# Lightning attention into a gated feed-forward: the state update of block 1 moved behind the second attention output group, its decayed k made in two pieces

## The chip, the cores and the metric

The kernel runs on one core of a Trainium2 chip. The metric is the device time of one execution in microseconds (us). A core has five engines that run their own instruction streams in order and wait for one another by semaphores: TensorE (PE in the profile, its weight loads PEld), VectorE (DVE), ScalarE (ACT), GpSimd (POOL) and SyncE (SP). Here POOL also issues all loads from memory, and SP the output stores and the transposing transfers.

## The reference

Causal linear attention with a decay per head, then a feed-forward layer with a sigmoid gate. There are 4 batches, 8 heads, 768 positions, head width 64. The reference walks over the positions in blocks of 64 and carries a state of 64 x 64 per batch and head:

```
intra    = (qb kb^T * Dmask) vb          # Dmask[i,j] = lam^(i-j), j <= i
inter    = (qb * lam^(i+1)) kv_state
out      = intra + inter
kb_dec   = kb * lam^(block-1-pos)
kv_state = lam^block * kv_state + kb_dec^T vb
```

The attention output, laid out as 3072 tokens x 512, goes through `(sigmoid(x Wg) * (x Wv)) Wo` with 1536 hidden columns. The output is 3072 x 512 in float32.

## The kernel before, in words

The kernel takes blocks of 128 positions (C = 128), so there are six steps n = 0 to 5, and each handles all four batches: 512 tokens. All matrix work is in bf16, accumulated in float32. Work is written by hand as a list of pieces; on every engine the instructions run in exactly the order in which the pieces are written (`manual_schedule`), so the order of the calls is the schedule.

For one step the pieces are these. `load` brings q, k, v into the tiles Q, K, V (POOL issues; L84 in blocks 0 and 1, where k and q arrive per pair of batches, L78 for q and k of later blocks). `t` transposes q and k: for block 1 on PE (L159), then q is scaled by the decay into QS on DVE (L185) and k copied into KS by ACT (L223); from block 2 on, the transposes are transfers that SP issues (L176) into QR and KR. `sc` makes the scores q kT for two batches (L235), and `m` multiplies them by the decay mask on DVE (L252). `a` makes the attention output for one pair of batches: the part from the state `Sb` (L268), the part inside the block (L256), and two copies by ACT into XT, the feed-forward's input (L282). `make_kd` multiplies k by its decay on POOL (L300 for blocks 0 and 1, L306 later). `fade` makes the decayed old state `SD` on POOL (L315). `c` updates the state of one pair of batches: 16 small matmuls (L330) of the decayed k with v into a PSUM tile `cp`, then DVE adds `SD` and writes `Sb` (L337; a plain copy, L335, in block 0). `gv` is one of the twelve 128-column slices of the feed-forward's first layer: four matmuls for the gate (L346), a sigmoid on ACT (L349), four matmuls for the value (L352), and their product on DVE (L355). `gvh` is the same for half of the tokens, that is for one pair of batches (L363, L366, L369, L373). `piece_po` is the second layer for one batch (L391), copied by ACT and stored by SP.

PSUM has two rotating sets of banks: five (`ps_at`, tag "ps") for attention pieces, three (`ps_ff`, tag "ff") for the feed-forward. The update of batches 0 and 1 takes its `cp` from the first set, that of batches 2 and 3 from the second, where it stands in line with the gate and value tiles of `gvh`: a new tile of that set waits for the reader of the tile three places before it.

Feed-forward pieces of step n are interleaved with attention pieces of step n+1, to keep PE busy while other engines finish. Around the change (L462 to L490) that is: five `gv` of block 0; state update of block 0; `fade` and `make_kd(1)`; more `gv` of block 0 with the attention of block 1's first pair; the state update of that pair, `c(1, 0)`; the last `gv` of block 0; then the attention of the second pair, between `gvh` pieces of the first. POOL's own order there is: loads of block 1, the output weights, `fade`, `make_kd(1)`, loads of block 2, `fade`, `make_kd(2)`, loads of block 3. So whatever `make_kd(1)` waits for holds up the loads of block 2 behind it. Block 1's k of batches 2 and 3 is loaded by a transfer of its own (`load(1, "qk", 2, 4)`).

Of the kernel before, what the change touches and what calls it, by code (L numbers as in the profile page):

```python
# [11 lines left out]
ALU = mybir.AluOpType  # L12
# [4 lines left out]
def kernel(  # L17
# [11 lines left out]
    nc = tc.nc  # L29

    B, H, S, D = q.shape
# [8 lines left out]
    NB2 = B // 2  # L40
# [28 lines left out]
    Q, K, V = {}, {}, {}  # L69
# [68 lines left out]
    kds = const.tile([128, H], FP32, tag="kds")  # L138
# [5 lines left out]
    for u in range(2):  # L144
        nc.vector.tensor_tensor(
            out=mask[:, u].rearrange("p (e x) c -> p e x c", e=2),
            in0=tri.unsqueeze(1).unsqueeze(1).to_broadcast([128, 2, 2, C]),
            in1=pk.rearrange("p (x u e) -> p u e x", u=2, e=2)[:, u].unsqueeze(3).to_broadcast([128, 2, 2, C]),
            op=ALU.mult)

    def half(e):
        return slice(e * 64, (e + 1) * 64)

    def head(g, u):
        return 4 * (g % 2) + 2 * u + g // 2
# [12 lines left out]
    QS, KS, MT, XT, KD = {}, {}, {}, {}, {}  # L168
# [128 lines left out]
    def make_kd(n):  # L297
        if n < 2:
            KD[n] = kdp.tile([128, B, H, D], BF16, tag="kd", name="kd")
            nc.gpsimd.tensor_tensor(  # L300
                out=KD[n], in0=K[n],
                in1=kds.unsqueeze(1).unsqueeze(3).to_broadcast([128, B, H, D]), op=ALU.mult)
            return
        KD[n] = kdp.tile([128, 2, B, HP, D], BF16, tag="kd", name="kd")
        for e in range(2):
            nc.gpsimd.tensor_tensor(  # L306
                out=KD[n][:, e], in0=K[n][:, e],
                in1=kds[:, e::2].unsqueeze(1).unsqueeze(3).to_broadcast([128, B, HP, D]), op=ALU.mult)
# [10 lines left out]
    def kdh(n, b, h):  # L319
        return KD[n][:, b, h, :] if n < 2 else KD[n][:, h % 2, b, h // 2, :]  # L320

    def c(n, *pairs):
        for bp in pairs:
            pool, tag = (ps_at, "ps") if bp == 0 else (ps_ff, "ff")
            cp = pool.tile([128, 2, HP, D], FP32, name="cp", tag=tag)
            for i in range(2):
                for hp in range(HP):
                    for u in range(2):
                        h = head(hp, u)
                        nc.tensor.matmul(cp[half(u), i, hp, :], lhsT=kdh(n, 2 * bp + i, h),  # L330
                                         rhs=V[n][:, 2 * bp + i, h, :], start=(i == 0 and hp == 0),
                                         stop=(i == 1 and hp == HP - 1), skip_group_check=True)
            dst = Sb[:, 2 * bp:2 * bp + 2]
            if n == 0:
                nc.vector.tensor_copy(dst, cp)  # L335
            else:
                nc.vector.tensor_tensor(out=dst, in0=cp, in1=SD.pop(bp), op=ALU.add)  # L337
# [90 lines left out]
    idle(2)  # L428

    make_kd(0)  # L430
    load_gv(3, GW)
    load(1, "qk", 0, 2)
# [18 lines left out]
    def a(n, *pairs):  # L451
        piece_a(n, pairs)

    def gv(n, *fts):
        for ft in fts:
            piece_gv(n, ft)

    def gvh(n, i, *fts):
        for ft in fts:
            piece_gvh(n, ft, i)  # L460

    gv(0, 0, 1, 2, 3, 4)  # L462
    c(0, 0, 1)
    fade()
    make_kd(1)
    gv(0, 5, 6, 7)
    t(1, 0)
# [3 lines left out]
    m(1, 0)  # L471
    gv(0, 10)
    a(1, 0)
    c(1, 0)
    gv(0, 11)
    t(1, 1)
    load(2, "qkv", 0, B)
# [4 lines left out]
    m(1, 1)  # L482
    gvh(1, 0, 3, 4)
    a(1, 1)
    c(1, 1)
    gvh(1, 0, 5, 6)
    fade()
    make_kd(2)
    load(3, "qkv", 0, B)
    gvh(1, 1, 0, 1, 2, 3, 4, 5, 6)  # L490
# [78 lines left out]
```

## Time and profile before

| | |
|---|---|
| median of 3 runs | 237.29 us (237.27 to 238.55) |
| the profiled execution | 237.51 us, of which its span is 235.7 us |
| PE busy | 223.4 us (95% of the span) |
| DVE / ACT / POOL busy | 95.5 / 80.5 / 81.7 us |
| mean granted TensorE clock | 0.986 of full speed |

The profile is of one execution. Its times count from the start of the span; the execution's own time is 1.81 us longer than the span. The page lists for each engine its busy time, shows the span in 40 slices of 5.9 us, and follows the chain of work that ended last backwards. Queries on the trace give the chain in order of time, the instructions in order of time with the idle time before them and its releaser in square brackets, and the busy time and granted clock in any stretch. In the order of time each matmul is drawn with its whole passage through the array, so that successive groups overlap; in the chain each group counts from the end of the one before.

### The profile page before, as it was taken

What the parts mean: (1) busy time and instruction counts of PE and PEld (TensorE: products, weight loads), DVE (VectorE), ACT (ScalarE), POOL (GpSimd) and SP (SyncE); (2) the same over time, 40 slices, a digit from 0 to 9 for tenths busy, and PEclk for the clock granted to TensorE, in tenths of its full rate; (3) what the DMA queues carried; (4) which work ended last, traced back from release to release, by engine and by line L of the source; (5) the groups of instructions that cost most, each with busy time, mean ns of one, the idle gap of its engine ahead of it and who ended that gap; (6) DMA issues with size and microseconds to landing.
All of it is one profiled execution on the core that took longest, in us unless ns stands there. A gap on an engine that the chain in (4) does not pass through costs nothing.

```text
span 235.7 us, 4288 instructions
## 1 busy us (share of the span) xinstructions
PE 223.4 (95%) x1790; PEld 112.1 (48%) x1790; DVE 95.5 (41%) x157; ACT 80.5 (34%) x147; POOL 81.7 (35%) x76
## 2 busy tenths in 40 slices
PE   7789999299999999999999999999999999999994
PEld 2444454158844445544445444446444445444442
DVE  3362547138534053233671334771243770243300
ACT  5653343034432212533323433314333315433221
POOL 8999984991970000793000891000000000000000
PEclk9999999689999999999999999999999999999999
DMA  8999999999999322299902299912370012100022
GB/s 54 144 179 177 164 191 157 204 173 158 126 184 151 92 92 89 85 182 155 114 26 92 85 176 154 96 49 92 92 132 0 3 44 92 44 0 0 0 92 89
DMA packets 102595, 24.92 MB, mean 106 GB/s; under 512 B 91696, under 2 KB 99632, under 8 KB 102576
## 3 DMA queue, kind: packets, MB, share of 16 engines
q0 software_dynamic: 82192, 14.16, 87.0%
q1 hardware_dynamic: 20384, 10.49, 18.4%
q8 instruction: 14, 0.23, 0.4%
q14 instruction: 5, 0.04, 0.1%
HBM read 28.32 MB, written 6.29 MB: 147 GB/s over the span
## 4 chain that ended last, share of the span: by engine, by line
PE 79%; POOL 13%; DMA 5%; issue 1%; DVE 0%; POOLq 0%
PE po L391 26%; PE gp L346 20%; PE vp L352 20%; DMA kb<-in_k_dram 5%; POOL kd L300 3%; PE gp L363 3%; PE vp L369 3%; PE sp L235 2%; PE op L256 2%; POOL qb L84 2%; POOL WV L91 2%; POOL WG L90 2%; POOL vb L84 2%; POOL kb L84 1%; PE po L380 1%; PE op L268 1%
## 5 line engine op out<-in xcount | busy, mean ns | idle before, releaser
L355 DVE TENSOR_TENSOR ht<-sg,vp 128x512 bf16<-128x512 bf16 x65 | 44.7, 688 | 80.0 <-PE vp L352 80.0
L346 PE MATMUL gp<-XT,WG 128*128 128x512 bf16 x260 | 67.7, 383 | 0.8 <-DMA WG<-in_moe_w_gate_dram 0.8
L352 PE MATMUL vp<-XT,WV 128*128 128x512 bf16 x260 | 67.6, 383 | 0.0
L349 ACT ACTIVATE sg<-gp 128x512 bf16<-128x512 f32 x65 | 38.8, 597 | 78.0 <-PE gp L346 78.0
L391 PE MATMUL po<-WO,ht 128*128 128x512 bf16 x276 | 61.9, 379 | 0.0
L391 PEld LDWEIGHTS <-ht 128*128 128x128 bf16 x276 | 26.3, 98 | 31.2
L352 PEld LDWEIGHTS <-WV 128*128 128x128 bf16 x260 | 25.5, 99 | 31.6 <-issue 1.1
L346 PEld LDWEIGHTS <-WG 128*128 128x128 bf16 x260 | 24.9, 98 | 30.8 <-DMA WG<-in_moe_w_gate_dram 1.3
L252 DVE TENSOR_TENSOR MT<-sp,mask 128x512 bf16<-128x512 f32 x44 | 27.8, 683 | 14.8 <-PE sp L235 14.8
L394 ACT COPY ob<-po 128x512 f32<-128x512 f32 x23 | 13.5, 586 | 52.5 <-PE po L391 50.6
L315 POOL TENSOR_TENSOR sd<-Sb,dec 128x512 f32<-128x512 bf16 x8 | 8.2, 1044 | 54.6 <-DVE Sb L337 54.6
L337 DVE TENSOR_TENSOR Sb<-cp,sd 128x512 bf16<-128x512 f32 x8 | 5.3, 688 | 20.9 <-PE cp L330 20.9
L84 POOL DMA_DIRECT2D vb<-in_v_dram x9 | 12.2, 1367 | 0.0
L282 ACT CAST XT<-op 128x512 bf16<-128x512 f32 x20 | 10.4, 597 | 3.0 <-PE op L256 3.0
L306 POOL TENSOR_TENSOR kd<-kb,kds 128x1024 bf16<-128x1024 bf16 x6 | 11.3, 1905 | 0.0
L165 PE MATMUL wm<-zero 128*128 128x512 bf16 x26 | 8.7, 469 | 1.2 <-DVE zero L103 1.2
L78 POOL DMA_DIRECT2D qb<-in_q_dram x8 | 9.4, 1184 | 0.0
L78 POOL DMA_DIRECT2D kb<-in_k_dram x8 | 9.2, 1167 | 0.0
L300 POOL TENSOR_TENSOR kd<-kb,kds 128x2048 bf16<-128x2048 bf16 x2 | 7.3, 3629 | 4.0 <-DMA kb<-in_k_dram 3.9
L363 PE MATMUL gp<-XT,WG 128*128 128x256 bf16 x56 | 8.4, 273 | 0.0
L369 PE MATMUL vp<-XT,WV 128*128 128x256 bf16 x56 | 8.4, 272 | 0.0
L330 PE MATMUL cp<-vb,kd 128*64 128x64 bf16 x160 | 3.8, 201 | 4.7 <-POOL kd L300 4.7
(59 smaller groups left out, 126.3 us busy)
## 6 DMA issues: line engine op xcount, KB each, us to landing
out_dram<-ob SPq DMA_DIRECT2D x23, 256.0 KB, 2.0
kb<-in_k_dram POOLq DMA_DIRECT2D x12, 256.0 KB, 8.8
qb<-in_q_dram POOLq DMA_DIRECT2D x11, 256.0 KB, 7.4
vb<-in_v_dram POOLq DMA_DIRECT2D x4, 512.0 KB, 11.5
WG<-in_moe_w_gate_dram POOLq DMA_DIRECT2D x6, 256.0 KB, 7.2
WV<-in_moe_w_val_dram POOLq DMA_DIRECT2D x6, 256.0 KB, 7.8
WO<-in_moe_w_out_dram POOLq DMA_DIRECT2D x3, 512.0 KB, 14.7
vb<-in_v_dram POOLq DMA_DIRECT2D x3, 256.0 KB, 10.3
```

The source lines that it names most:

```text
L78: nc.gpsimd.dma_start(out=lst[n][:, e].rearrange("p b y d -> p (b y) d"), in_=src[:, e::2, sl, :].rearrange("b y s d -> s (b y) d"))
L84: nc.gpsimd.dma_start(out=lst[n][:, b0:b1], in_=src[b0:b1, :, sl, :].rearrange("b h s d -> s (b h) d"))
L252: nc.vector.tensor_tensor(out=MT[n, b][:, u], in0=SP[n, b][u], in1=mask[:, u], op=ALU.mult)
L300: nc.gpsimd.tensor_tensor(out=KD[n], in0=K[n], in1=kds.unsqueeze(1).unsqueeze(3).to_broadcast([128, B, H, D]), op=ALU.mult)
L346: nc.tensor.matmul(gp, lhsT=WG[:, mt, fs], rhs=x[:, mt, :], start=(mt == 0), stop=(mt == NMT - 1))
L349: nc.scalar.activation(sg, gp, AF.Sigmoid)
L352: nc.tensor.matmul(vp, lhsT=WV[:, mt, fs], rhs=x[:, mt, :], start=(mt == 0), stop=(mt == NMT - 1))
L355: nc.vector.tensor_mul(HT[n, ft], sg, vp)
L363: nc.tensor.matmul(gp[:, cs], lhsT=WG[:, mt, fs], rhs=x[:, mt, cs], start=(mt == 0), stop=(mt == NMT - 1))
L369: nc.tensor.matmul(vp[:, cs], lhsT=WV[:, mt, fs], rhs=x[:, mt, cs], start=(mt == 0), stop=(mt == NMT - 1))
L391: nc.tensor.matmul(po, lhsT=HT[n, ft][:, tt * 128:(tt + 1) * 128], rhs=WO[:, ft, :], start=(ft == 0), stop=(ft == NFT - 1))
L394: nc.scalar.copy(ob, po)
```

## The change

`c(1, 0)`, which stood between the attention output of the first pair of block 1 and the last `gv` of block 0, is taken from there. At the place where `c(1, 1)` stood, behind the attention output of the second pair, both pairs are now updated: `c(1, 0, 1)`. Its instructions are the same ones as before, in another place. `make_kd` makes the decayed k of blocks 0 and 1 with two POOL instructions, each for two batches, instead of one for all four. Nothing else is changed.

```diff
     def make_kd(n):
         if n < 2:
             KD[n] = kdp.tile([128, B, H, D], BF16, tag="kd", name="kd")
-            nc.gpsimd.tensor_tensor(
-                out=KD[n], in0=K[n],
-                in1=kds.unsqueeze(1).unsqueeze(3).to_broadcast([128, B, H, D]), op=ALU.mult)
+            for bp in range(NB2):
+                bs = slice(2 * bp, 2 * bp + 2)
+                nc.gpsimd.tensor_tensor(
+                    out=KD[n][:, bs], in0=K[n][:, bs],
+                    in1=kds.unsqueeze(1).unsqueeze(3).to_broadcast([128, 2, H, D]), op=ALU.mult)
             return
...
     m(1, 0)
     gv(0, 10)
     a(1, 0)
-    c(1, 0)
     gv(0, 11)
     t(1, 1)
     load(2, "qkv", 0, B)
...
     m(1, 1)
     gvh(1, 0, 3, 4)
     a(1, 1)
-    c(1, 1)
+    c(1, 0, 1)
     gvh(1, 0, 5, 6)
     fade()
     make_kd(2)
```

## The prediction

> **What bounds the kernel now.** I read the slices first, to see where TensorE (PE) is not busy or not at full clock.
>
> ```profile
> PE   7789999299999999999999999999999999999994
> ...
> PEclk9999999689999999999999999999999999999999
> ```
>
> Each digit is a slice of 5.9 us. From the fourth slice to the last but one PE is busy throughout, but for one slice: the eighth (41 to 47 us), with a 2, and there and in the next the granted clock is down as well. So PE sets the end, and there is one hole in it. The chain in order of time (start, length, what) tells what the hole consists of.
>
> ```profile
> 30.09 11.69 DMA kb<-in_k_dram
> ...
> 41.84 3.63 POOL kd L300
> ...
> 45.51 0.64 PE cp L330 x16
> 46.15 1.82 PE gp L346 x4
> 47.97 1.66 PE vp L352 x4
> 49.64 0.57 PE tq L159 x16
> 50.20 0.45 PE tk L159 x16
> 50.65 0.54 PE gp L363 x4
> ...
> 56.83 0.25 PE cp L330 x16
> 57.08 0.54 PE gp L363 x4
> 57.63 0.44 PE vp L369 x4
> ```
>
> Read downwards: the load of block 1's second half of k, issued at 30.09, lands at 41.78; POOL then makes the decayed k of all four batches until 45.47; only then can PE start c(1, 0), though that update reads batches 0 and 1 alone. Behind it PE runs slowly: the four gate matmuls of gv(0, 11) take 1.82. The busy times in these stretches (PE, PEld, DVE, ACT, POOL, then clock, DMA share, GB/s) confirm both halves of the loss.
>
> ```profile
> 40.78:45.51 4.73, 0.00 (x0) 0.00 (x0) 0.00 (x0) 0.89 (x2) 3.67 (x2) 0.70 1.45 199
> 45.51:50.65 5.14, 5.14 (x57) 2.53 (x58) 1.60 (x3) 0.60 (x1) 5.14 (x5) 0.62 1.56 192
> 50.65:57.08 6.43, 6.43 (x105) 5.22 (x106) 4.70 (x10) 3.26 (x7) 2.15 (x2) 1.00 2.45 157
> 57.08:235.70 178.62, 175.26 (x1278) 87.18 (x1276) 69.54 (x110) 57.86 (x104) 35.15 (x26) 1.00 0.83 88
> ```
>
> PE stands still for 4.73 us with no DVE work either, then works 5.14 us at a mean clock of 0.62. From 50.65 on it has clock 1.00 and no holes; the last stretch misses 3.36 us of PE only, which is the tail after its last matmul. Whatever is saved before 57.08 therefore moves the rest forward as a block, unless a load or another engine cannot follow.
>
> **The change part by part.** First, what PE can do at 40.78, when a(1, 0) has left it:
>
> ```profile
> 40.14 0.64 PE L256 MATMUL op<-MT,vb 128*64 128x128 bf16 x16
> ```
>
> Without c(1, 0) the next instructions are gv(0, 11), whose inputs are older, and t(1, 1), whose k must have landed. Their full-speed prices come from the same pieces in the same surroundings elsewhere in the chain: a gate group behind small matmuls, a value group, and a double update.
>
> ```profile
> 117.50 0.97 PE gp L346 x4
> 118.47 0.86 PE vp L352 x4
> ...
> 94.75 0.51 PE cp L330 x32
> ```
>
> gv(0, 11) is 0.97 + 0.86 = 1.83, t(1, 1) is 0.57 + 0.45 = 1.02 as now. From 50.65 to 56.83 PE already ran at full clock, so these pieces keep their 6.18. The update of both pairs is 0.51. Laid end to end from 40.78: 1.83 + 1.02 + 6.18 + 0.51 = 9.54, so the double update ends at 50.32 where c(1, 1) now ends at 57.08. **That is 6.76 us saved.** Of this 4.73 is the stand, and the rest, 2.03, is what the low clock cost: c, gate and value took 0.64 + 1.82 + 1.66 = 4.12 against some 0.26 + 1.83, half of the double update and gv(0, 11).
>
> The Trainium skill, "TensorE: Matmul & The Clock Gate", section "What's actually happening", says that PE drops to half clock after about 3.4 us idle and comes back after about 3.4 us of sustained work. By that alone the drop would cost an estimated half of 3.4, 1.7 us, and the sum below would come out at 231.2 rather than 230.9. The trace agrees in kind (0.62 after a stand of 4.73), and the rows decide the size.
>
> Second, whether the waits that were hidden behind the stand now show. PE reaches the transposes of k at 40.78 + 1.83 + 0.57 = 43.18; k lands at 41.78, so 1.4 us are to spare. The split of make_kd acts on block 0 too, ahead of this load in POOL's order, and two instructions are longer than one:
>
> ```profile
> 17.48 3.64 POOL L300 TENSOR_TENSOR kd<-kb,kds 128x2048 bf16<-128x2048 bf16 x1
> ...
> 41.84 3.62 POOL L300 TENSOR_TENSOR kd<-kb,kds 128x2048 bf16<-128x2048 bf16 x1 [3.94 <-DMA kb<-in_k_dram]
> 45.40 2.37 POOL L78 DMA_DIRECT2D qb<-in_q_dram  x2
> ...
> 58.97 3.78 POOL L306 TENSOR_TENSOR kd<-kb,kds 128x1024 bf16<-128x1024 bf16 x2
> ```
>
> Two of half the size take 3.78 against 3.64, so the loads of block 1 go out 0.14 later; the 1.4 covers that at no cost. In block 1 the first piece runs while POOL now idles 3.94 us, and the second from 41.84 for about 1.9 to 43.7. The double update wants it at 40.78 + 1.83 + 1.02 + 6.18 = 49.81, six microseconds later; without this cover a wait there would cost its length. If the first piece waited for all of k, both would be done at 45.6, still in time. v of the second half, issued just behind k, is needed by a(1, 1) about 49.2:
>
> ```profile
> 31.22 1.23 POOL L84 DMA_DIRECT2D vb<-in_v_dram  x1
> ...
> vb<-in_v_dram POOLq DMA_DIRECT2D x1, 256.0 KB, 11.8
> ```
>
> It lands at 43.0. The loads of block 2 are behind make_kd(1) on POOL; they start at 43.7 instead of 45.40, 1.7 earlier. SP's queue has the same entries in the same order.
>
> Third, what the double update queues up. c(1, 0) was one DVE addition at a place where DVE was idle; now two stand back to back, and behind them the products of gvh. On PE the tile of batches 2 and 3 is in the set of three banks, and the gate of gvh(1, 0, 6) takes over its bank. Now, in order of time:
>
> ```profile
> 56.67 0.42 PE L330 MATMUL cp<-vb,kd 128*64 128x64 bf16 x16
> 57.20 0.69 DVE L337 TENSOR_TENSOR Sb<-cp,sd 128x512 bf16<-128x512 f32 x1 [0.53 <-PE cp L330]
> 57.46 0.60 PE L369 MATMUL vp<-XT,WV 128*128 128x256 bf16 x4
> 57.94 0.60 PE L363 MATMUL gp<-XT,WG 128*128 128x256 bf16 x4
> ...
> 95.12 1.29 DVE L337 TENSOR_TENSOR Sb<-cp,sd 128x512 bf16<-128x512 f32 x2 [4.94 <-PE cp L330]
> ```
>
> DVE starts 0.53 after the update's first matmul; one addition ends at 57.89, and the gate starts at 57.94, 0.05 later. Without a wait it would start 0.44 (the usual step) after 57.46, at 57.90: so 0.04 is waited already. After the change the update's first matmul comes 7.02 earlier than 56.67 (56.83 less 49.81), at 49.65; the pair of additions takes 1.29 and ends at 49.65 + 0.53 + 1.29 = 51.47, and the bank is free at 51.52. The gate could start at 57.90 - 6.76 = 51.14. It waits 0.38, which is **0.34 us more than now**. The bounds are 0 (the first update's sixteen matmuls let DVE start earlier) and 1.29 (the whole pair); I take 0.34, the value by position.
>
> In the set of five banks c(1, 0) moves from before the tiles of t(1, 1) to behind those of a(1, 1), so each tile between takes the bank one place earlier. Counting back five tiles, the readers are the masks of block 1's first pair, the two copies of a(1, 0) and the readers of t(1, 1), each done over a microsecond before the taker: no cost. The extra wait of fade for the first pair's state costs nothing on PE; POOL is then at the end of block 2's loads, and only make_kd(2) and block 3's loads are queued behind it, with PE's uses of them in the second half of the next block.
>
> The sum: 6.76 - 0.34 = 6.42. Against the profiled execution that is 237.51 - 6.42 = 231.09 (span 235.7 - 6.42 = 229.3). The median is 0.22 below the profiled execution, so my figure is **230.9 us**.
>
> **The rivals.** *A wait moves into t(1, 1).* PE waits there for k itself rather than for the decayed k. For it: the load is in one queue with the weights and took 11.69. Against it: the 1.4 us to spare. If k landed 2 us later than PE gets there, the time would be 232.9. The clock would hold, as it did over the short stand at block 0's first gate, whose four matmuls took 1.04 straight after:
>
> ```profile
> 18.00 1.04 PE L346 MATMUL gp<-XT,WG 128*128 128x512 bf16 x4 [0.82 <-DMA WG<-in_moe_w_gate_dram]
> ```
>
> Up to 1.29 at the bank of gvh is of this kind too: 231.9.
>
> *The time is won and lost again in block 2.* PE arrives 6.4 earlier at the first scores of block 2, but their transposed k comes from transfers which start only 1.7 earlier.
>
> ```profile
> 61.40 3.50 SPq L176 DMA_TRANSPOSE KR<-kb  x1
> ...
> DMA to landing us min/median/max: 7.8/7.8/7.8
> ...
> 84.01 0.62 PE L235 MATMUL sp<-QS,KR 64*128 64x128 bf16 x16
> ```
>
> It lands at 69.2, and PE now asks at 84.01, after the change at 77.6: 8.4 to spare even if the transfer starts no earlier. A partial loss, say k landing at 80.0, would give 233.3.
>
> *Slower than before*, by the same place: earlier loads of block 2 meet the output weights, and the transposing transfer lands so late that PE stands past the limit and falls to the low clock again (2.03). It breaks even when the wait is 6.42 - 2.03 = 4.39, a landing at 82.0; at 86.0 the wait is 8.4 and the time 230.9 + 8.4 + 2.0 = 241.3. That needs a landing 12.8 us later than in this trace, with nothing pointing to it.
>
> *The change doesn't do what it says*: should both pieces of the decayed k be tied to some later event, or the order on PE stay, the time is 237.3. The order of calls is the order on each engine, which speaks against it.
>
> **How the numbers follow.** Forecast as worked out, 0.82 (230.2 to 231.6, from the gate's wait at its bounds and the spread of the two near runs); a residual wait in t(1, 1), at the bank or in part in block 2, between 231.6 and 234.9, 0.10; no change, 0.04; slower, 0.04. The range 229.8 to 233.1 adds to the low end some 0.2 for a gate group at 0.86 instead of 0.97 and the run's spread, and reaches to the 2 us wait in t(1, 1) above; it leaves out under 2 in 10. By the bound of 1% (2.4 us), which is about what a measurement of this kernel can tell from no change: faster 0.92, same 0.04, slower 0.04.
>
> **What would show it.** In the profile after, the eighth slice of PE reads 9 and its clock does too; the wait of L330 for L300 is gone; gv(0, 11) runs from about 40.8 and takes 1.8; L330 appears as one group of 32 near 49.7, with two additions back to back behind it and the gate two groups later starting near 51.5; the first scores of block 2 stand near 77.6 with nothing waiting; the span is about 229.3. I am wrong if a stand remains between 40 and 52 us, if the clock is below 1.00 after 40, or if PE waits for k or its transpose at L159 or L235.

## The result and the profile after

The changed kernel takes 230.88 us (median of four, 230.31 to 231.89) against 237.42 for the kernel before on the same chip: a ratio of 0.972, 95% interval 0.967 to 0.977. The forecast was 230.9. The profiled execution of the changed kernel took 231.89 with a span of 230.1.

The page of the changed kernel shows PE's eighth slice filled and its clock whole from the fourth slice on:

```profile
PE   7689999999999999999999999999999999999994
...
PEclk9979999999999999999999999999999999999999
```

The chain in order of time, same columns as before (start, length, what). In the changed kernel the gate is L348, the value L354, the update L332; of gvh, gate and value are L365 and L371.

```profile
41.19 0.57 PE op L256 x16
41.76 0.16 issue
41.91 0.81 PE gp L348 x3
42.73 0.86 PE vp L354 x4
...
44.16 0.45 PE tk L159 x16
...
50.78 0.51 PE cp L332 x32
51.29 0.54 PE gp L365 x4
51.83 0.44 PE vp L371 x4
52.27 0.04 issue
52.30 0.60 PE gp L365 x4
```

a(1, 0) ends at 41.76 and the double update at 51.29 (one gate matmul's record is missing behind 41.76, which the chain calls "issue"). Busy times and clock in that stretch and in the rest:

```profile
41.76:51.29 9.53, 9.38 (x160) 7.10 (x162) 5.67 (x12) 5.00 (x11) 7.61 (x6) 1.00 1.49 197
51.29:230.10 178.81, 174.29 (x1257) 87.14 (x1276) 69.92 (x111) 57.63 (x103) 36.73 (x28) 1.00 1.01 95
```

9.53 us at clock 1.00, where the kernel before needed 16.30 (40.78 to 57.08): 6.77 won. The rest takes 178.81 against 178.62: 0.19 given back. The span is nevertheless only 5.6 shorter, because in this execution a(1, 0) ended 0.98 later than in the profile of before. That arose in block 0, where the clock was at half for 3.41 us, which shows in the page's third slice, a 7, and in the second of these windows:

```profile
9.56:12.97 3.41, 1.97 (x41) 1.24 (x42) 1.29 (x2) 1.99 (x5) 3.41 (x5) 1.00 2.44 155
12.97:16.39 3.42, 3.11 (x30) 1.52 (x30) 2.35 (x5) 0.97 (x2) 1.93 (x4) 0.50 1.87 180
```

From 11.5 to 17.3 us the kernel before has clock 1.00. The lateness isn't the change's: the first instruction that the change touches, block 0's decayed k on POOL, starts only at 18.97 here, and a second profile of the changed kernel (below) does not have it.

POOL in order of time, with idle time and releaser in brackets:

```profile
39.65 1.89 POOL L302 TENSOR_TENSOR kd<-kb,kds 128x1024 bf16<-128x1024 bf16 x1
43.68 1.90 POOL L302 TENSOR_TENSOR kd<-kb,kds 128x1024 bf16<-128x1024 bf16 x1 [2.14 <-DMA kb<-in_k_dram]
```

The first piece of the decayed k is made while the second half of k is still on its way. PE's update, at 50.78, waits for neither.

### The profile page after: what moved, and what is told of

Its sections match the earlier page's. It is cut to its first block, busy times and chain, and to the rows that moved or that the text cites. A ratio compares the mean times of both kernels' runs of the same rounds, so it can differ in the third digit from the quotient of the medians.

```text
span 230.1 us, 4267 instructions
## 1 busy us (share of the span) xinstructions
PE 220.9 (96%) x1766; PEld 112.1 (49%) x1790; DVE 95.3 (41%) x157; ACT 80.5 (35%) x147; POOL 81.9 (36%) x78
## 4 chain that ended last, share of the span: by engine, by line
PE 92%; DMA 3%; POOL 2%; issue 1%; DVE 0%; POOLq 0%
PE po L393 26%; PE gp L348 25%; PE vp L354 24%; DMA qb<-in_q_dram 3%; PE sp L235 3%; PE gp L365 3%; PE op L256 3%; PE vp L371 3%; PE op L268 1%; PE wm L165 1%; PE cp L332 1%; PE po L382 1%; POOL kb L84 1%; PE tq L159 1%; PE tk L159 0%
## 5 line engine op out<-in xcount | busy, mean ns | idle before, releaser
L348 PE MATMUL gp<-XT,WG 128*128 128x512 bf16 x252 | 66.2, 379 | 0.7 <-issue 0.2
L354 PE MATMUL vp<-XT,WV 128*128 128x512 bf16 x256 | 65.9, 379 | 0.0
L354 PEld LDWEIGHTS <-WV 128*128 128x128 bf16 x260 | 25.4, 98 | 30.7
L348 PEld LDWEIGHTS <-WG 128*128 128x128 bf16 x260 | 24.8, 98 | 29.5 <-issue 0.3
L308 POOL TENSOR_TENSOR kd<-kb,kds 128x1024 bf16<-128x1024 bf16 x6 | 11.3, 1905 | 4.0 <-DMA kb<-in_k_dram 4.0
L365 PE MATMUL gp<-XT,WG 128*128 128x256 bf16 x56 | 8.4, 273 | 0.0
L371 PE MATMUL vp<-XT,WV 128*128 128x256 bf16 x56 | 8.4, 272 | 0.0
L302 POOL TENSOR_TENSOR kd<-kb,kds 128x1024 bf16<-128x1024 bf16 x4 | 7.6, 1912 | 2.1 <-DMA kb<-in_k_dram 2.1
L375 DVE TENSOR_TENSOR ht<-sg,vp 128x256 bf16<-128x256 bf16 x14 | 5.8, 419 | 5.1 <-PE vp L371 4.1
```

Source lines behind the costliest of these rows:

```text
L348: nc.tensor.matmul(gp, lhsT=WG[:, mt, fs], rhs=x[:, mt, :], start=(mt == 0), stop=(mt == NMT - 1))
L354: nc.tensor.matmul(vp, lhsT=WV[:, mt, fs], rhs=x[:, mt, :], start=(mt == 0), stop=(mt == NMT - 1))
L365: nc.tensor.matmul(gp[:, cs], lhsT=WG[:, mt, fs], rhs=x[:, mt, cs], start=(mt == 0), stop=(mt == NMT - 1))
L371: nc.tensor.matmul(vp[:, cs], lhsT=WV[:, mt, fs], rhs=x[:, mt, cs], start=(mt == 0), stop=(mt == NMT - 1))
```

## The experiments

**The changed kernel again**, as a measure for what ran with it.

> The changed kernel once more, as the measure for the others on this chip: 230.9 us, with a gap of 0.3 to 0.4 us ahead of the gate behind the double addition and 0.5 to 1.5 us to spare between the landing of k and its transposes on PE.

Measured: 230.47 us (229.87 to 231.07), ratio 0.968 (0.965 to 0.971). Its chain:

```profile
40.10 0.57 PE op L256 x16
...
43.07 0.45 PE tk L159 x16
...
49.70 0.51 PE cp L332 x32
50.20 0.54 PE gp L365 x4
...
51.18 0.04 issue
51.21 0.60 PE gp L365 x4
```

```profile
41.92 1.90 POOL L302 TENSOR_TENSOR kd<-kb,kds 128x1024 bf16<-128x1024 bf16 x1 [2.08 <-DMA kb<-in_k_dram]
43.77 2.37 POOL L78 DMA_DIRECT2D qb<-in_q_dram  x2
```

From a(1, 0) to the end of the double update it is again 9.54 (40.67 to 50.21). k is there by 41.92 and PE's transposes of it start at 43.07: 1.15 to spare. In the first profile it was 44.16 less 43.68, 0.48, both inside what was expected. The gate behind the additions comes 0.04 late and lasts 0.60 instead of 0.44: a wait of 0.20, below what was expected.

**The move without the split.**

```diff
-            for bp in range(NB2):
-                bs = slice(2 * bp, 2 * bp + 2)
-                nc.gpsimd.tensor_tensor(out=KD[n][:, bs], ...)     # two batches each
+            nc.gpsimd.tensor_tensor(out=KD[n], ...)                # all four
```

> The double update behind the second attention group, the decayed k still made by one POOL instruction. Theory (the stand goes because PE meets the update only at about 49.8 us, when even the whole decayed k, done near 45.5, is ready): the whole gain, 230.9 us, no wait of the update for the decayed k, the gate two groups behind the additions still waiting 0.3 to 0.4. Rival (the split carries the gain): the update waits for the decayed k and the time is at least 233.

Measured: 231.25 us (230.57 to 231.91), ratio 0.972 (0.968 to 0.976). POOL in this kernel makes all of the decayed k from 42.03, and the next load follows at 45.59; the chain has the update 4.6 us after that.

```profile
42.03 3.62 POOL L300 TENSOR_TENSOR kd<-kb,kds 128x2048 bf16<-128x2048 bf16 x1 [4.00 <-DMA kb<-in_k_dram]
45.59 2.37 POOL L78 DMA_DIRECT2D qb<-in_q_dram  x2
```

```profile
50.23 0.50 PE cp L330 x32
```

From a(1, 0) to the end of the double update it is 9.53 here too (41.20 to 50.73), and the times overlap with those of the change (230.57 to 231.91 against 229.87 to 231.07). So the move alone carries the gain; the split isn't needed for it. The gate behind the additions waits 0.20 as in the change, not the 0.3 to 0.4 expected.

**The split without the move.**

```diff
     a(1, 0)
+    c(1, 0)
     gv(0, 11)
...
-    c(1, 0, 1)
+    c(1, 1)
```

> The decayed k made in two pieces, the update of the first pair left in its old place ahead of the last slice of block 0. Theory (the stand was a wait for the wrong pair's k): the first piece is done near 40, PE asks for it near 40.8, so the stand and the low clock go here too and, with no pair of additions, the wait at the bank as well: 230.5 us, 0.3 under the change. Rival (the order carries the gain): the stand of 4.7 stays, 237.4 us. Between them, if the first piece is late by up to 1 us on POOL: 231.5, clock 1.00.

Measured: 230.43 us (230.16 to 231.37), ratio 0.969 (0.966 to 0.972): no difference from the change that these runs can tell. Its chain and one line of its waits:

```profile
38.41 1.86 POOL kd L302
40.27 0.04 issue
40.32 0.44 PE cp L332 x16
40.76 0.97 PE gp L348 x4
```

```profile
PE cp L332 <- POOL kd L302: 0.2, 1, 0.2
```

The first piece is ready at 40.27, and PE waited 0.2 for it; the low clock is gone (gate 0.97 instead of 1.82). So each half of the change removes the stand by itself: the move, because PE asks later; the split, because PE asks for a piece that doesn't depend on the late load. Together they do no more than one. What differs is the slack: here PE comes 0.2 too early, while in the move alone the decayed k is done 4.6 before the update asks for it (45.65 to 50.23).

**The two pairs in the other order.**

```diff
-    c(1, 0, 1)
+    c(1, 1, 0)
```

> The change with the two pairs of the double update in the other order, batches 2 and 3 first. Theory (0.34 us is lost because the gate takes the bank of the second of two additions): the addition that frees the bank is now the first, the gate does not wait, 0.3 us less than the change, 230.5 us; visible in the trace rather than in the time. Rival (the gate waits for something else): the same 0.35 stays and the time is that of the change.

Measured: 230.23 us (230.03 to 231.89), ratio 0.969 (0.966 to 0.973). The time tells nothing at this size; the chain does:

```profile
50.56 0.51 PE cp L332 x32
51.07 0.54 PE gp L365 x4
51.61 0.44 PE vp L371 x4
52.05 0.44 PE gp L365 x4
```

The gate follows without a gap and lasts 0.44. So the small wait did come from the bank that the second of two additions frees.

**Filling the stand of the kernel before with idle matmuls**, which separates the stand from the low clock.

```diff
     a(1, 0)
+    filler(21)      # 21 matmuls of zeros into a PSUM tile of the feed-forward's set
     c(1, 0)
```

> The kernel before, with 21 matmuls of zeros (about 0.216 us each, 4.5 us in all) put on PE where it stands, ahead of the first pair's update; their product is not used. Theory (6.76 is 4.73 of stand and 2.03 of low clock that follows from it): the update still starts near 45.5, but the clock is 1.00 behind it, gv(0, 11) takes about 1.8 instead of 3.5, and the time is 237.4 - 2.0 = 235.4 us. Rival (the low clock comes from something else at that place, loads or transposes): gv(0, 11) still takes 3.5 and the time stays at 237.4.

Measured: 235.88 us (235.52 to 236.33) against 237.98 for before, ratio 0.990 (0.987 to 0.994). Chain, and the window behind the filling:

```profile
46.19 0.44 PE cp L330 x16
46.64 0.97 PE gp L346 x4
```

```profile
46.20:48.47 2.27, 2.27 (x26) 1.10 (x28) 0.69 (x1) 0.60 (x1) 2.27 (x3) 1.00 1.25 208
```

The update starts as late as before and the clock is whole: 2.1 us come back without a single wait removed. From the first update to the end of c(1, 1), the trace has 9.72 (46.19 to 55.91) against 11.57 (45.51 to 57.08): 1.85 is the low clock. The remaining 0.18 of the forecast's 2.03 goes with the stand: behind a wait, at full clock, the sixteen update matmuls count 0.44 in the chain, because there no earlier group covers their drawn passage through the array, and without a wait 0.25 (`c(1, 1)`, at 56.83 in the chain before). Joining the two updates saves nothing by itself, as 0.51 is twice that.

**The load of k later**, to see what PE pays once the spare time is used up. Three positions in POOL's order: behind v, behind v and the first third of the output weights, and behind all of these weights.

```diff
-    load(1, "qk", 2, 4)
+    load(1, "q", 2, 4)
     load(1, "v", 2, 4)
+    load(1, "k", 2, 4)            # k_after_v
     load_wo(0, NFT // 3)          # the loop over the weights, written out
                                   # k_after_wo1: here instead
     load_wo(1, NFT // 3)
     load_wo(2, NFT // 3)
                                   # k_after_wo3: here instead
```

> The change with the load of k of batches 2 and 3 put behind that of v only. It should land 0.5 to 1.5 us later, near 42.5 to 43.3; PE had 0.4 to 1.2 us to spare there. Theory (PE waits only for what exceeds the slack): a stand of 0 to 0.8 us, clock 1.00, 230.5 to 231.3 us. Rival (the slack is none, as the landing moves with the queue): 1.5 us stand, 232 us.

> The change, with the load of k of batches 2 and 3 put behind that of v and behind the first third of the output weights. It should land some 3 to 4 us later, near 45 to 46, and PE waits for it at its transposes for the lateness less what was to spare (0.5 to 1.4 us): a stand of 2 to 3.5 us. Theory (a short stand costs its length alone): 232.9 to 234.4 us, clock 1.00 afterwards. Rival (any stand of this kind drops the clock): 2 us more than the stand.

> The change, with the load of k of batches 2 and 3 put behind that of v and all of the output weights. It should land near 51, so PE stands about 8 us at its transposes. Theory (a long stand costs its length and about 2 us of low clock): 230.9 + 8 + 2 = 241 us, slower than the kernel before, with the clock near 0.5 to 0.6 for some 4 us behind the stand. Rival (the lateness is partly hidden, since the work of block 1 can be reordered by the engine or the load overlaps better): under 238.

Measured: 231.19, 235.23 and 240.65 us; ratios to before 0.971 (0.968 to 0.973), 0.988 (0.983 to 0.993), 1.011 (1.007 to 1.015). PE in order of time, one fence for each kernel, with the wait in brackets:

```profile
43.17 0.64 PE L159 MATMUL tk<-ident,kb 128*64 128x128 bf16 x16 [0.46 <-DMA kb<-in_k_dram]
43.74 0.61 PE L365 MATMUL gp<-XT,WG 128*128 128x256 bf16 x4
```

```profile
45.70 0.73 PE L159 MATMUL tk<-ident,kb 128*64 128x128 bf16 x16 [2.73 <-DMA kb<-in_k_dram]
46.36 1.03 PE L365 MATMUL gp<-XT,WG 128*128 128x256 bf16 x4
```

```profile
50.92 1.07 PE L159 MATMUL tk<-ident,kb 128*64 128x128 bf16 x16 [8.66 <-DMA kb<-in_k_dram]
51.92 1.04 PE L365 MATMUL gp<-XT,WG 128*128 128x256 bf16 x4
```

A stand of 0.46 costs little more than its length: from the transposes of k to the end of the double update it is 7.32 (43.17 to 50.49) where the change needs 7.14 (43.07 to 50.21), and the 0.18 is again that the first group behind a wait counts longer. One of 8.66 costs more than that, and makes the kernel slower than before: there it is 9.85 (50.92 to 60.77), 2.53 more than behind the short stand, from the low clock. But one of 2.73 also drops the clock. The expectation had it whole there; the gate matmuls take 1.03 instead of 0.61, and the windows say when:

```profile
42.69:46.11 3.42, 0.69 (x24) 0.53 (x21) 1.11 (x2) 0.00 (x0) 0.39 (x1) 1.00 1.76 189
46.11:49.52 3.41, 3.41 (x25) 2.33 (x20) 0.42 (x1) 1.73 (x3) 3.41 (x3) 0.50 1.12 185
```

The clock is whole through the stand and falls at 46.11, when PE is at work again. From the transposes to the end of the double update it is 8.80 (45.70 to 54.50): 1.48 lost to the clock.

**How short a stand drops the clock.** Two explanations were left: that a stand under 3 us is enough, or that the transposes on both sides of this one do not count as work, which would lengthen it past 3.4. The Trainium skill, "TensorE: Matmul & The Clock Gate", section "Part 4: PE-mode transpose", says that a transpose doesn't count as busy in the same way. The kernel before with less filling puts a stand between ordinary matmuls, and the late load was run a second time.

```diff
-    filler(21)
+    filler(11)      # fill_half;  fill_most: filler(16)
```

> The kernel before with 11 instead of 21 matmuls of zeros ahead of the first pair's update; their product is not used. The stand behind them is 2.2 to 2.9 us, with ordinary matmuls on both sides. Theory A (only a stand of about 3.4 us drops the clock; the drop behind the 2.7 us stand at the transposes came from the transposes not counting as work): clock 1.00 and gv(0, 11) 1.8 us, 235.6 us. Theory B (a stand of 2 to 3 us is enough by itself): clock near 0.6 behind it, 236.5 to 238 us.

> The same with 16 matmuls of zeros: a stand of 1.1 to 1.8 us. Theory A: clock 1.00, 235.6 us. Theory B with a limit near 2: clock 1.00 as well, 235.6 us; a clock under 1.00 here would put the limit under 1.8 us.

> The change with the load of k behind v and the first third of the output weights, once more: whether the low clock behind a stand of 2.7 us is there again. Theory B: a stand of 2 to 3 us, then 1.5 to 1.8 us lost to a clock near 0.5 to 0.6, 234 to 235.5 us. If the drop depends on when the stand falls: clock 1.00 this time and 233.3 us, and times spread by 1.7 us between executions.

Measured: 237.31 us (ratio 0.998, interval 0.995 to 1.000), 235.87 (0.992, 0.989 to 0.995), and 234.72 (0.984, 0.981 to 0.987). PE in order of time, in this order:

```profile
45.77 0.64 PE L330 MATMUL cp<-vb,kd 128*64 128x64 bf16 x16 [3.13 <-POOL kd L300]
46.35 1.89 PE L346 MATMUL gp<-XT,WG 128*128 128x512 bf16 x4
```

```profile
45.76 0.44 PE L330 MATMUL cp<-vb,kd 128*64 128x64 bf16 x16 [1.22 <-POOL kd L300]
46.13 1.04 PE L346 MATMUL gp<-XT,WG 128*128 128x512 bf16 x4
```

```profile
45.68 1.06 PE L159 MATMUL tk<-ident,kb 128*64 128x128 bf16 x16 [3.02 <-DMA kb<-in_k_dram]
```

Behind 3.13 us between ordinary matmuls the gate takes 1.89, as behind the full stand; behind 1.22 it takes 1.04. So transposes aren't needed for the drop. It is also not certain each time: of the eight executions with the load behind the first third of the weights six have a mean clock of 0.985 to 0.993 and 234.66 to 236.59 us, the two others 1.000 and 233.78 and 233.49. With 11 filling matmuls nine of ten have 0.986 to 0.993, one 0.997 with 236.02 us. With 16, eight of ten have 0.997 or more; the two below (0.990 and 0.993, at 238.06 and 237.69 us) have no profile, so whether it was this stand that cost them is open. The mean clock is a rough guide, as it falls for any low stretch: 3 of the 30 executions of the change, its two halves, the swapped pairs and the shortest late load have 0.993 too, one of them the first profile with its low stretch in block 0.

The traces show a third explanation that fits better than either. In all thirteen profiles the granted clock changes only at points that lie whole multiples of 3.41 us apart, from a start that differs between executions, and the low stretches within the kernel last 3.41, 6.83 or 10.24. Cut at these points, the kernel before reads:

```profile
39.23:42.64 3.41, 1.55 (x35) 0.83 (x33) 1.49 (x3) 1.48 (x3) 0.80 (x1) 1.00 2.09 174
42.64:46.05 3.41, 0.54 (x16) 0.51 (x16) 0.00 (x0) 0.00 (x0) 3.41 (x2) 0.50 1.24 207
46.05:49.47 3.42, 3.42 (x12) 1.04 (x8) 0.69 (x1) 0.60 (x1) 3.42 (x4) 0.50 1.36 199
```

The clock fell 1.86 us into the stand, behind a window in which PE had worked 1.55 of 3.41 us. Ahead of the other drops it had worked 0.00 (load behind all weights), 0.69 and 0.96 (behind the first third), 0.73 (11 filling matmuls) and, in block 0 of the first profile after, 1.97; with 16 filling matmuls it worked 2.19 in the window with the stand, and the clock stayed. While the clock was whole, no window with 2.04 or more was followed by a drop, and of those with less only two at the very start, with 1.90 and 1.91, were not. So it is the work of PE in such a window, more than the stand's length, that goes with the drop, and where the windows lie would explain why one kernel loses the clock in some executions only. That last point is argued: no run here set their place.

No version here beats the change by more than the runs tell apart: 230.47 for the change, 230.43 and 230.23 for the split alone and the swapped pairs.

## Why the prediction was right, point by point

**The stand and the low clock (6.76).** 6.77 measured (16.30 against 9.53), and the pieces laid end to end took 9.53 and 9.54 where the sum said 9.54. The division was nearly right: 4.73 stand, 1.85 clock, and 0.18 for the longer first group behind a stand, which the forecast had put under the clock. Filling the stand gave the clock's part separately: 2.1 us in the time. The 1.7 us estimated from the Trainium skill's rule comes near the 1.85; the trace has PE at half clock from 45.51 to 49.47, 3.96 us.

**The bank behind two additions (0.34).** The mechanism was right, as the swapped order showed, and the size was off: the gate waits 0.20 (0.04 + 0.60 - 0.44) against 0.03 before, so 0.17 more. The step that failed is the release 1.34 after the first addition's start (1.29 and 0.05). In the trace after, the additions and the gate stand so:

```profile
51.15 1.29 DVE L339 TENSOR_TENSOR Sb<-cp,sd 128x512 bf16<-128x512 f32 x2 [0.64 <-PE cp L332]
...
52.30 0.60 PE L365 MATMUL gp<-XT,WG 128*128 128x256 bf16 x4
```

The gate starts 1.15 after them, 0.14 before the pair's drawn end. The first addition also began 0.53 after the first update matmul (50.62), as forecast.

**The agreement of the total.** That the median came within 0.02 us of the forecast is luck. The bank term was 0.17 too large, the four executions spread over 1.6 us, and the second measurement has 230.47, 7.60 below its kernel before, where the first has 6.54 and the forecast 6.42. What the runs confirm is the mechanism, and a gain of about that size.

**The hidden waits.** k was in time for its transposes with 0.48 and 1.15 to spare, instead of 1.4; the loads of block 2 went out at 43.77 in the second profile, forecast 43.7. Neither piece of kd nor v held PE. In block 2 nothing came late (the first scores at 77.28 in the second profile, forecast 77.6): the rest of the kernel is longer by the bank's wait alone, so that rival and the slower one got nothing. That a landing late enough would make it slower by stand and clock together is real, as the load behind all weights showed with 240.65, 2.7 above before; it took a stand of 8.66 us.

**What was wrong in the working of a rival.** I priced a wait of 2 us at the transposes at its length, "the clock would hold", from a stand of 0.82. Stands of 2.73, 3.02 and 3.13 in the profiles show that this can't be carried over so far: they cost 1.4 to 1.7 us more than their length, most times. The rival didn't occur, so the forecast wasn't touched, but its price was too low if the stand had been nearer 3 than 1. In the rival that ends slower, the landing 12.8 us later is the one that breaks even (82.0 less 69.2); the one priced at 241.3 is 16.8 later (86.0).

**The halves of the change.** The prediction put the whole gain on the move and used the split only as harmless. The runs show that either would do. Nothing in the profile after could have shown that, since both are in it.

## What to carry to other kernels

When an engine stands, look at what the waiting instruction really reads: here it waited for the decayed k of four batches and needed two, so either asking later or making the piece separately removed the whole stand. Count what a TensorE stand costs with the clock that follows, since the stands of 2.73 to 4.73 us cost 1.4 to 2.0 more than their length, and idle matmuls that fill it get that part back even when the wait itself can't be removed. Before moving a step, lay the remaining pieces end to end from the moment the engine is free, at the prices of undisturbed neighbours, and then check each input's landing against the new times: here that sum was right to 0.01 us in the trace, though the times of single executions spread far more.

## What the runs showed of the hardware that was not expected

The clock fell behind stands of 2.73, 3.02 and 3.13 us, and not behind 0.46 or 1.22 in the profiles; the Trainium skill, "TensorE: Matmul & The Clock Gate", section "What's actually happening", puts the limit at one idle window of about 3.4. The traces agree with the window's length, as the clock changes on a grid of 3.41 us, but the window need not be idle: PE had worked 1.55 of 3.41 us ahead of the drop in the kernel before, and 1.97 ahead of the one in block 0, where its longest wait was 0.88. The drop comes at the end of such a window, wherever the stand is by then: 1.86 us into it in the kernel before, and 0.41 after PE had resumed behind the 2.73 us stand. And of two additions back to back on VectorE, the tile read by the second was free 0.14 us before the pair's drawn end (0.13 to 0.14 in four profiles), whereas a single addition let the next gate start 0.05 after its end.
